# Sums of exponentials in the v products by constant columns beside v, and cluster masks of five score tiles on VectorE

## The chip, the cores and the metric

The kernel runs on one core of a Trainium2 chip. The metric is the device time of one execution in microseconds (us), the median of several runs. Traces come from one profiled execution. TensorE (PE) multiplies matrices, VectorE (DVE), ScalarE (ACT) and GpSimd (POOL) work on elements, SyncE (SP) and ScalarE issue DMAs.

## The reference

Attention restricted to clusters, and then a feed-forward layer. There are 4 batches, 8 heads, 768 positions, 64 values per head and 16 centroids per head.

```python
q_assign = argmax(q_n @ c_n)          # nearest of 16 centroids, per query
k_assign = argmax(k_n @ c_n)          # and per key
mask   = q_assign[..., :, None] == k_assign[..., None, :]
scores = where(mask, scale * (q @ k.T), -1e9)
attn   = exp(scores - max); attn = attn / (sum(attn) + 1e-9)
x      = (attn @ v) laid out as (3072 tokens, 512)
h = x @ w_in                          # 512 x 2048
out = (maximum(h, 0) ** 2) @ w_out    # 2048 x 512
```

## The kernel before

**Pairs of heads.** The attention part is a loop over `p`, 16 pairs of heads (4 batches x 4 pairs; `NG` is 16). The two heads of a pair are `e` = 0 and 1. Scores are kept transposed: keys on the 128 partitions, queries along the free axis. A pair has nine score tiles. Tiles 0 to 5 are the six blocks of 128 keys against the first 512 queries (`QA`), each for both heads, so 128x1024 numbers. Tiles 6 to 8 hold two key blocks each against the last 256 queries (`QB`). Score tiles stand in PSUM, in a pool `ps_sc` of three buffers that are reused in turn.

**A score tile.** `tile_of` takes a buffer (`begin`), issues the mask matmuls (`mask`, L450), which add nothing where the clusters of key and query agree and a huge negative number where they don't, adds the score matmuls on top (`score`, L441), and ScalarE takes the exponential into `ex` (`exponential`, L457). The operands of the mask matmuls are three bfloat16 rows per head (`rows_of`), made by VectorE in `number` from the logits to the centroids (`logits`, L329, and `turn_logits`, L340), sent to DRAM as `far` and read back (L377, L380).

**The v products.** `times_v` (L475) multiplies each block of keys' exponentials by v: the stationary operand is v of one head, 128 keys x 64, and the moving operand is `ex`, 128 keys x 512 or 256 queries. Head 0 writes to PSUM partitions 0 to 63 and head 1 to 64 to 127 of one bank, `V` for the first 512 queries and `M` for the last 256. ScalarE copies both into `xT` (`evict`, L484).

**The sums.** VectorE adds the nine tiles of exponentials into `total` (`add`, L460). TensorE multiplies `total` by a column of ones scaled by `UP` (`add_up`, L494), which sums over the keys. VectorE turns that and takes the reciprocal (`invert`, L503, L507), SP sends it to DRAM and reads it back broadcast over partitions (`far_r`, L509, and `rb`, L516), and VectorE multiplies `xT` by it in the next pair (`finish`, L539).

**What else runs in a pair.** q and k of later pairs are loaded, split into 16-bit words by ScalarE (`split_words`, L309), stored, and read back by a transposing DMA into `qkT` (`turn_words`, L321). One block of weights is loaded and rounded by ScalarE, VectorE and GpSimd (`round_1` to `round_3`).

**Order.** The order on every engine is written out by hand in the loop over `p` (`manual_schedule`): each engine executes what it is given in the order of the code. So an instruction that waits holds up all that stands behind it on its engine. SP's DMAs are such a queue too. Within a pair TensorE runs the nine score tiles, the products into `V`, those into `M`, the logits of a later pair, and the ones-matmuls.

**After the attention part.** The feed-forward layer follows, built from seven products in place of eight at up to two levels (L793, L883, L1003, L1111). It begins at 318.9 us of the trace. The last pair's sums are inverted and applied there, in `Rounding.behind`.

Of the kernel before, what the change touches and what calls it, by code (L numbers as in the profile page):

```python
# [25 lines left out]
def kernel(  # L26
# [40 lines left out]
    loads_v = att.enter_context(tc.tile_pool(name="loads_v", bufs=2))  # L67
    qktp = att.enter_context(tc.tile_pool(name="qktp", bufs=3))
    small = att.enter_context(tc.tile_pool(name="small", bufs=2))
    once = att.enter_context(tc.tile_pool(name="once", bufs=1))  # L70
    expp = att.enter_context(tc.tile_pool(name="expp", bufs=9))
    accp = att.enter_context(tc.tile_pool(name="accp", bufs=1))
# [6 lines left out]
    raw = {}  # L79
    raw_v = {}  # L80
# [13 lines left out]
    def load_v(pair):  # L94
        if pair >= NG:
            return
        b, hp = divmod(pair, HP)
        raw_v[pair] = loads_v.tile([P, 2, NCH, D], F32, name="v_raw")
        nc.sync.dma_start(
            raw_v[pair], v[b, 2 * hp : 2 * hp + 2].rearrange("h (p j) d -> p h j d", p=P)  # L100
        )
# [115 lines left out]

    seen = const.tile([P, NG * NBL], F32, name="seen")

    oh = accp.tile([P, NBL, 2, D], BF16, name="oh", tag="part")  # L220
# [120 lines left out]

    def number(pair):
        n = 2 * NBL
        mx = small.tile([P, n], F32, name="mx")
        best = once.tile([P, n, C], BF16, name="best")
        src = lt.pop(pair)

        def over_c(t):
            return t.unsqueeze(2).to_broadcast([P, n, C])

        nc.vector.reduce_max(out=mx, in_=src, axis=AX.X)
        nc.vector.tensor_tensor(out=best, in0=src, in1=over_c(mx), op=ALU.is_ge)
        nc.vector.tensor_tensor(
            out=best, in0=best, in1=order.unsqueeze(1).to_broadcast([P, n, C]), op=ALU.mult
        )
        nc.vector.reduce_max(out=mx, in_=best, axis=AX.X)
        if pair == 0:
            nc.vector.tensor_tensor(
                out=oh.rearrange("p b e c -> p (b e) c")[:, :, 0:C], in0=best, in1=over_c(mx),
                op=ALU.is_equal,  # L360
            )
            return
        squared = small.tile([P, n], F32, name="squared")
        nc.vector.tensor_tensor(out=squared, in0=mx, in1=mx, op=ALU.mult)
        for i, of in enumerate((squared, mx, squared)):
            nc.vector.tensor_scalar(
                out=marks[:, i, 0:n].rearrange("p (e b) -> p b e", e=2),
                in0=of.rearrange("p (b e) -> p b e", e=2), scalar1=factor[:, i : i + 1],
                scalar2=None if i == 1 else constant[:, i : i + 1], op0=ALU.mult,
                **({} if i == 1 else {"op1": ALU.add}),  # L370
            )
        turned = small.tile([P, 3, 32], BF16, name="marks_t")
        nc.vector.transpose(
            out=turned.rearrange("p f i -> p (f i)"), in_=marks.rearrange("p f i -> p (f i)")
        )
        far = dram.tile([3, 4, 32, 32], BF16, name="far")
        nc.sync.dma_start(far.rearrange("f g r i -> (g r) f i"), turned)  # L377
        rows = ohT[pair] = rows_of[pair % 2]
        for e in range(2):
            nc.sync.dma_start(  # L380
                rows[D * e : D * e + 3].rearrange("f w (g n) -> f (w g) n", g=2),
                far[:, :, NBL * e : NBL * (e + 1)].rearrange("f g b i -> f g (b i)"),
            )

# [35 lines left out]
    total = {}  # L420
    part = {}
# [14 lines left out]
    def score(pair, i, j, first):  # L436
        n = columns(i)
        c, cols = spots(i)[j]
        for e in range(2):
            rows = slice(D * e, D * (e + 1))  # L440
            nc.tensor.matmul(  # L441
                sc[i][:, e, cols], lhsT=qkT[pair][rows, NCH + c],
                rhs=qkT[pair][rows, n.start // P : n.stop // P], start=first, stop=not first,
            )
# [14 lines left out]
    def add(eng, out, a, b):  # L459
        eng.tensor_tensor(out=out, in0=a, in1=b, op=ALU.add)  # L460

# [9 lines left out]
    def times_v(pair, i, bank):  # L471
        n = columns(i)
        for c, cols in spots(i):
            for e in range(2):
                nc.tensor.matmul(  # L475
                    bank[D * e : D * (e + 1), 0 : n.stop - n.start], lhsT=raw_v[pair][:, e, c],
                    rhs=ex[i][:, e, cols], start=c == 0, stop=c == NCH - 1,
                )
        ex.pop(i)

    def evict(pair, i, bank):
        b, hp = divmod(pair, HP)
        n = columns(i)
        nc.scalar.copy(out=x_of(b)[:, hp, n], in_=bank[:, 0 : n.stop - n.start])  # L484

    spread_out = {}
    reciprocals = {}
    sums = {}

    def add_up(pair, bank):  # L490
        rows = P // 4
        for e in range(2):
            for g in range(2):
                nc.tensor.matmul(  # L494
                    bank[rows * (2 * e + g) : rows * (2 * e + g + 1), 0:TB], lhsT=ups[:, 0:rows],
                    rhs=total[pair][:, e, TB * g : TB * (g + 1)], start=True, stop=True,
                )
        total.pop(pair)
        sums[pair] = bank

    def invert(pair):
        turned = endp.tile([P, NBL, 32], F32, name="sums_t")
        nc.vector.transpose(  # L503
            out=turned.rearrange("p b i -> p (b i)"), in_=sums.pop(pair)[:, 0:TB]
        )
        r = seen[:, NBL * pair : NBL * (pair + 1)]
        nc.vector.reciprocal(out=r, in_=turned[:, :, 0])  # L507
        far = dram.tile([2, P // 2, NBL], F32, name="far_r")
        nc.sync.dma_start(far.rearrange("e i b -> (e i) b"), r)  # L509
        reciprocals[pair] = far  # L510

    def spread(pair):
        far = reciprocals.pop(pair)
        rb = endp.tile([P, 2, 32, NBL], F32, name="rb")
        for e in range(2):
            nc.sync.dma_start(  # L516
                rb[D * e : D * (e + 1)].rearrange("p g i b -> p (g i b)"),
                far[e].rearrange("i b -> (i b)").partition_broadcast(D),
            )
        spread_out[pair] = [rb[:, g] for g in range(2)]  # L520


    def spread_last(pair):
        far = reciprocals.pop(pair)
        spread_out[pair] = []
        for g in range(2):
            rb = outp.tile([P, DM], F32, name="rb_last", tag="osb")[:, 0:TB]
            for e in range(2):
                nc.sync.dma_start(
                    rb[D * e : D * (e + 1)],  # L530
                    far[e, 32 * g : 32 * (g + 1)].rearrange("i b -> (i b)").partition_broadcast(D),
                )
            spread_out[pair].append(rb.rearrange("p (i b) -> p i b", i=32))

    def finish(pair):
        b, hp = divmod(pair, HP)
        x = x_of(b)[:, hp].rearrange("p (g b i) -> p g b i", g=2, b=NBL)
        for g in range(2):
            nc.vector.scalar_tensor_tensor(  # L539
                out=x[:, g], in0=x[:, g], scalar=UP,  # L540
                in1=spread_out[pair][g].rearrange("p i b -> p b i"),
                op0=ALU.mult, op1=ALU.mult,
            )
        spread_out.pop(pair)
# [21 lines left out]
    def w_sums(i, odd=0):  # L566
# [8 lines left out]
        return a, s1, s2, s3, s4  # L575

# [36 lines left out]
    for p in range(NG):  # L613
# [3 lines left out]
        if p == HP + 1:  # L617
            nc.sync.dma_start(x_far[FEED[3]], xT.pop(FEED[3]))
        if p:
            invert(p - 1)  # L620
            if p == NG - 1:
                early_x_sums()
            turn_words(p + 2)
            spread(p - 1)
# [4 lines left out]
        if p:  # L629
            load_ahead(p - 1)  # L630

# [15 lines left out]
        else:  # L647
            for i in range(NB):
                tile_of(p, i)
        total[p] = endp.tile([P, 2, S], F32, name="total")  # L650
        first, last = total[p][:, :, 0:QA], total[p][:, :, QA:S]
        add(nc.vector, first, ex[0], ex[1])
# [6 lines left out]
        add(nc.vector, first, first, ex[2])  # L659
        for i in range(NB, NCH):  # L660
            if p != 1 or i > NB:
                tile_of(p, i)
            add(nc.vector, first, first, ex[i])
# [4 lines left out]
        else:  # L668
            split_words(p + 3, 0)
# [4 lines left out]
        part = accp.tile([P, 2, 512], F32, name="part")  # L674
        add(nc.vector, part, ex[NCH], ex[NCH + 1])
        add(nc.vector, part, part, ex[NCH + 2])
        add(nc.vector, last, part[:, :, 0:QB], part[:, :, QB : 2 * QB])
# [8 lines left out]
        round_1(p)  # L686


        for i in range(NCH):
            times_v(p, i, V)  # L690
        evict(p, 0, V)
        for i in range(NCH, NCH + NB):
            times_v(p, i, M)
        raw_v.pop(p)
        if p + 1 < NG:
            bank = begin("ls")
            if 2 < p + 2:
                if p + 2 < NG:
                    logits(p + 2, bank)
            add_up(p, bank[:, 1])  # L700
        evict(p, NCH, M)
# [630 lines left out]
    class Rounding:  # L1332
# [27 lines left out]
        def behind(self, i):  # L1360
            nonlocal wtp, spare_tile, four_r
            if i == 0:
                add_up(NG - 1, bank_tile(TB))
                invert(NG - 1)
                spread_last(NG - 1)
            if i == F2 - 2:
                finish(NG - 1)
                nc.sync.dma_start(x_far[FEED[2]], xT.pop(FEED[2]))
            if i == 5:
# [242 lines left out]
```

## Time and profile before

| | |
|---|---|
| median of 3 runs | 878.6 us (878.52 to 878.69) |
| profiled execution, its own time | 878.45 us |
| its span in the trace | 876.7 us |
| TensorE busy | 869.9 us, 99% |
| VectorE busy | 754.3 us, 86% |
| ScalarE busy | 385.8 us, 44% |
| GpSimd busy | 181.7 us, 21% |
| granted TensorE clock | 0.999 of full |
| from the first v product to the feed-forward part | 24.47 to 318.91 us |
| DMA engines busy in that stretch | 0.67 |

Busy times are sums over one execution. The span is what the trace covers; the execution's own time is 1.75 us longer. A row of the timeline gives a start, a duration, the engine, the line of the kernel, the operation, output and inputs by name with their sizes, and how many such instructions follow each other. A matmul's float32 product appears as two hardware passes, so that the trace shows twice as many as the program issues. Their durations overlap, so the rate is read from differences of starts. A row of a group gives busy time, mean duration in ns of one, and the idle time of the engine ahead of them with what ended it.

### The profile page before, as it was taken

Reading aid. Unit: us, or ns where it says so; the run is one execution under the profiler, and the core shown is the slowest. Engines: PE = TensorE matmul, PEld = TensorE weight load, DVE = VectorE, ACT = ScalarE, POOL = GpSimd, SP = SyncE. Lnnn points to the kernel's source line nnn. Section 1 sums busy time; section 2 is a strip of 40 time slices with the busy share of each in tenths; the row PEclk is TensorE's granted clock in tenths of the full one; section 3 lists DMA queues with packets and bytes.
Section 4 is the critical chain, followed back from the end, with each engine's and each line's share of the span. In section 5 each row is a group of like instructions: output and inputs, shape, how many; then the busy total and the mean of one; then the engine's idle time right before and its main releaser. Section 6 shows DMA issues by size and latency. Waiting matters only on the chain.

```text
span 876.7 us, 14996 instructions
## 1 busy us (share of the span) xinstructions
PE 869.9 (99%) x5487; PEld 597.4 (68%) x5487; DVE 754.3 (86%) x1359; ACT 385.8 (44%) x621; POOL 181.7 (21%) x240
## 2 busy tenths in 40 slices
PE   9999999999999999999999999999999999999997
PEld 5444444444444455568866689997767987779997
DVE  6799888888888999999858996797899898997786
ACT  5877667777765657750035430002453005440000
POOL 0000010000000246740056300005550064510000
PEclk9999999999999999999999999999999999999999
DMA  7777886767764235226701347681024740138663
GB/s 253 179 190 193 220 267 179 201 188 194 202 167 127 82 136 172 94 91 225 285 25 43 102 145 208 196 259 37 31 79 155 235 128 25 37 122 247 166 203 121
DMA packets 166402, 136.05 MB, mean 155 GB/s; under 512 B 58826, under 2 KB 140082, under 8 KB 166066
## 3 DMA queue, kind: packets, MB, share of 16 engines
q1 hardware_dynamic: 148018, 119.00, 46.1%
q10 hardware_dynamic: 18304, 16.03, 5.9%
q8 instruction: 45, 0.74, 0.3%
q14 instruction: 35, 0.29, 0.1%
HBM read 82.10 MB, written 41.89 MB: 141 GB/s over the span
## 4 chain that ended last, share of the span: by engine, by line
PE 99%; DMA 0%; ACT 0%; DVE 0%; issue 0%
PE bank L793 28%; PE bank L1111 25%; PE sc L441 14%; PE av_a L475 10%; PE bank L1003 6%; PE av_b L475 5%; PE sc L450 4%; PE bank L883 3%; PE sc L329 1%; PE more L883 1%; PE sc L494 1%; PE more L873 1%; DMA q_raw<-in_q_dram 0%; PE av_a L289 0%; ACT ex L457 0%; PE sc L274 0%
## 5 line engine op out<-in xcount | busy, mean ns | idle before, releaser
L457 ACT ACTIVATE ex<-sc 128x1024 f32<-128x1024 f32 x144 | 144.3, 1026 | 37.5 <-PE sc L441 31.6
L441 PE MATMUL sc<-qkT 64*128 64x512 f32 (+1 forms) x768 | 150.5, 484 | 0.0
L988 DVE TENSOR_TENSOR g<-bank,g 128x384 f32<-128x384 f32 (+3 forms) x205 | 102.3, 515 | 21.1 <-PE bank L793 12.8
L769 ACT ACTIVATE g<-g 128x384 f32<-128x384 f32 x122 | 62.9, 516 | 93.7 <-DVE g L988 73.5
L441 PEld LDWEIGHTS sc<-qkT 64*128 64x128 f32 x768 | 65.6, 188 | 42.1 <-issue 30.2
L793 PE MATMUL bank<-xT,w_s 128*128 128x384 f32 x256 | 93.1, 486 | 0.0
L793 PE MATMUL bank<-x_t,w_s 128*128 128x384 f32 x256 | 93.0, 486 | 0.0
L1267 ACT COPY spare<-bank 128x128 f32<-128x128 f32 x35 | 9.3, 264 | 187.7 <-PE bank L1111 163.8
L475 PE MATMUL av_a<-ex,v_raw 128*64 128x512 f32 x384 | 85.9, 596 | 0.0
L460 DVE TENSOR_TENSOR total<-total,ex 128x1024 f32<-128x1024 f32 x64 | 78.7, 1229 | 6.5
L161 POOL TENSOR_TENSOR w_in<-w_in,w_raw 128x512 int32<-128x512 int32 x16 | 21.4, 1337 | 293.9 <-DVE w_in L153 293.9
L571 POOL TENSOR_TENSOR w_s<-w_in 128x256 f32<-128x256 f32 x32 | 25.6, 800 | 247.4 <-PE bank L1111 146.4
L1111 PE MATMUL bank<-home,l 128*128 128x128 f32 x560 | 74.0, 275 | 0.0
L793 PEld LDWEIGHTS bank<-xT,w_s 128*128 128x128 f32 x256 | 48.6, 190 | 34.2 <-issue 0.5
L1111 PEld LDWEIGHTS bank<-home,l 128*128 128x128 f32 x560 | 68.2, 192 | 0.0
L793 PEld LDWEIGHTS bank<-x_t,w_s 128*128 128x128 f32 x256 | 48.1, 190 | 29.1
L793 PE MATMUL bank<-xT,w_in 128*128 128x384 f32 x184 | 67.1, 487 | 0.0
L770 ACT ACTIVATE g<-g 128x384 f32<-128x384 f32 x122 | 63.8, 523 | 3.9
L475 PEld LDWEIGHTS av_a<-ex,v_raw 128*64 128x64 f32 x384 | 26.2, 137 | 51.0 <-issue 49.3
L450 PE MATMUL sc<-rows 64*128 64x512 bf16 (+1 forms) x360 | 58.8, 323 | 0.0
L793 PEld LDWEIGHTS bank<-xT,w_in 128*128 128x128 f32 x184 | 34.4, 190 | 21.7 <-DVE g L551 0.6
L1111 PE MATMUL bank<-home,g 128*128 128x128 f32 x352 | 46.5, 275 | 0.0
(221 smaller groups left out, 1557.9 us busy)
## 6 DMA issues: line engine op xcount, KB each, us to landing
home<-w_far SPq DMA_DIRECT2D x92, 256.0 KB
words<-flat SPq DMA_DIRECT2D x26, 384.0 KB
w_raw<-in_moe_w_in_dram SPq DMA_DIRECT2D x16, 512.0 KB
w_raw<-in_moe_w_out_dram SPq DMA_DIRECT2D x16, 512.0 KB
w_far<-home SPq DMA_DIRECT2D x28, 256.0 KB
g<-g_far SPq DMA_DIRECT2D x28, 256.0 KB
v_raw<-in_v_dram SPq DMA_DIRECT2D x16, 384.0 KB
g_far<-third SPq DMA_DIRECT2D x24, 256.0 KB
```

What stands on the lines that cost most here:

```text
L441: nc.tensor.matmul(sc[i][:, e, cols], lhsT=qkT[pair][rows, NCH + c], rhs=qkT[pair][rows, n.start // P : n.stop // P], start=first, stop=no ...
L450: nc.tensor.matmul(sc[i][:, e, cols], lhsT=ohT[pair][rows, 1, c * P : (c + 1) * P], rhs=ohT[pair][rows, 0, columns(i)], start=first, stop= ...
L457: nc.scalar.activation(out=ex[i], in_=sc.pop(i), func=ACT.Exp, scale=SCALE)
L460: eng.tensor_tensor(out=out, in0=a, in1=b, op=ALU.add)
L475: nc.tensor.matmul(bank[D * e : D * (e + 1), 0 : n.stop - n.start], lhsT=raw_v[pair][:, e, c], rhs=ex[i][:, e, cols], start=c == 0, stop=c ...
L769: nc.scalar.activation(out=to, in_=to, func=ACT.Relu)
L770: nc.scalar.square(to, to)
L793: nc.tensor.matmul(bank, lhsT=operands[j][0][:, kk], rhs=operands[j][1][:, kk], start=(kk == 0), stop=(kk == H2 - 1),)
L883: nc.tensor.matmul(bank, lhsT=left, rhs=right, start=True, stop=True)
L988: nc.vector.tensor_tensor(out=out, in0=one, in1=two, op=ALU.add)
L1003: nc.tensor.matmul(bank, lhsT=left[j][:, f], rhs=right(j)[:, f], start=(f == 0), stop=(f == F2 - 1),)
L1111: nc.tensor.matmul(bank, lhsT=left[:, f], rhs=rhs[:, f], start=(f == 0), stop=(f == F4 - 1))
```

## The change

The v tiles of two alternate pairs become fixed buffers, `v_ups`. In them the 64 columns of v of each block of keys stand beside 64 columns that hold the constant `UP`, set once by GpSimd. A v product now takes 128 columns as its stationary operand: 64 rows of its output are the product, and the other 64 all hold the sum of the exponentials. Each head gets its own output. For the first 512 queries that is a buffer of `ps_sc`, with two heads side by side; for the last 256 it is `M`. `V` is used for the logits. The additions on VectorE, `total`, `part` and the ones-matmuls are gone.

`evict` copies both outputs to a tile `outputs` in SBUF. One row of sums per head goes to DRAM (`store_sums`), is read back as 128x12 (`load_sums`), inverted, stored, and broadcast as before. `finish` multiplies the product rows by it, per head, into `xT`.

From pair 2 on, tiles 0 to 4 get no mask matmuls. VectorE multiplies their exponentials by a comparison of the query's cluster (`of_queries`, the cluster numbers broadcast over the partitions) with the key's (`clusters`, one number per partition), one instruction per head and tile. SP loads both from `far` in the pair before (`load_clusters`), and ScalarE scales the keys' numbers (`scale_clusters`). Tiles 5 to 8, and all tiles of pairs 0 and 1, are masked by TensorE as before.

In the order: the word split of one operand moves behind the exponential of tile 6; the reciprocal moves behind `number` and the loads of v and weights; the last pair's `finish` comes one step earlier in the feed-forward part.

```diff
-    loads_v = att.enter_context(tc.tile_pool(name="loads_v", bufs=2))
+    v_ups = [once.tile([P, 2 * NCH * P + P], F32, name=f"v_ups_{i}") for i in range(2)]
...
-        nc.sync.dma_start(
-            raw_v[pair], v[b, 2 * hp : 2 * hp + 2].rearrange("h (p j) d -> p h j d", p=P)
-        )
+        raw_v[pair] = v_ups[pair % 2]
+        for e in range(2):
+            at = e * (NCH * P + D)
+            halves = raw_v[pair][:, at : at + NCH * P].rearrange("p (c d) -> p c d", d=P)
+            nc.sync.dma_start(
+                halves[:, :, 0:D], v[b, 2 * hp + e].rearrange("(p j) d -> p j d", p=P)
+            )
...
+    for t in v_ups:
+        for at in (D, NCH * P):
+            in_front = t[:, at : at + NCH * P].rearrange("p (c d) -> p c d", d=P)
+            nc.gpsimd.memset(in_front[:, :, 0:D], UP)
...
+    def load_clusters(pair):
+        far = far_marks.pop(pair)
+        for e in range(2):
+            for g in range(2):
+                n = min(TB, QA - TB * g)
+                nc.sync.dma_start(
+                    of_queries[:, e, TB * g : TB * g + n],
+                    far[1, g, NBL * e : NBL * e + n // 32].rearrange("b i -> (b i)")
+                    .partition_broadcast(P),
+                )
+        of_keys[pair] = small.tile([P, 2 * HANDS], BF16, name="of_keys")
+        for e in range(2):
+            for g in range(2):
+                c = slice(NB * g, min(NB * (g + 1), HANDS))
+                nc.sync.dma_start(
+                    of_keys[pair][:, HANDS * e + c.start : HANDS * e + c.stop],
+                    far[1, 2 + g, NBL * e : NBL * e + P // 32 * (c.stop - c.start)]
+                    .rearrange("(c b) i -> (b i) c", b=P // 32),
+                )
+
+    def scale_clusters(pair):
+        clusters[pair] = small.tile([P, 2, HANDS], F32, name="clusters")
+        nc.scalar.activation(
+            out=clusters[pair].rearrange("p e c -> p (e c)"), in_=of_keys.pop(pair),
+            func=ACT.Copy, scale=0.5 / BIG,
+        )
...
-    def times_v(pair, i, bank):
-        n = columns(i)
+    def times_v(pair, i, e, bank):
         for c, cols in spots(i):
-            for e in range(2):
-                nc.tensor.matmul(
-                    bank[D * e : D * (e + 1), 0 : n.stop - n.start], lhsT=raw_v[pair][:, e, c],
-                    rhs=ex[i][:, e, cols], start=c == 0, stop=c == NCH - 1,
-                )
+            at = (e * NCH + c) * P
+            nc.tensor.matmul(
+                bank, lhsT=raw_v[pair][:, at : at + P], rhs=ex[i][:, e, cols],
+                start=c == 0, stop=c == NCH - 1,
+            )
...
-    def add_up(pair, bank):
...
+    def store_sums(pair):
+        sums[pair] = dram.tile([2, S], F32, name="sums")
         for e in range(2):
+            row = D * (1 - e)
+            nc.sync.dma_start(sums[pair][e : e + 1], outputs[pair][row : row + 1, e])
+
+    def load_sums(pair):
+        compact[pair] = small_c.tile([P, NBL], F32, name="compact")
+        nc.sync.dma_start(
+            compact[pair], sums.pop(pair).rearrange("e (i b) -> (e i) b", b=NBL)
+        )
...
+    def tile_by_hand(pair, i):
+        begin(i)
+        score(pair, i, 0, True, True)
+        exponential(i)
+        for e in range(2):
+            nc.vector.scalar_tensor_tensor(
+                out=ex[i][:, e], in0=of_queries[:, e], scalar=clusters[pair][:, e, i : i + 1],
+                in1=ex[i][:, e], op0=ALU.is_equal, op1=ALU.mult,
+            )
...
         if p:
-            invert(p - 1)
-            if p == NG - 1:
-                early_x_sums()
+            load_sums(p - 1)
             turn_words(p + 2)
-            spread(p - 1)
         if 2 < p + 1 < NG:
             turn_logits(p + 1)
             number(p + 1)
         load_v(p + 1)
         if p:
             load_ahead(p - 1)
+
+        if p:
+            invert(p - 1)
+            spread(p - 1)
...
+        if BY_HAND <= p + 1 < NG:
+            load_clusters(p + 1)
+
+        bank = begin("av")
+        for i in range(NCH):
+            for e in range(2):
+                times_v(p, i, e, bank[:, e])
         round_1(p)
...
+        evict(p, slice(0, QA), sc.pop("av"))
+        both = M.rearrange("p (e n) -> p e n", e=2)
+        for e in range(2):
+            for i in range(NCH, NCH + NB):
+                times_v(p, i, e, both[:, e])
+        ex.clear()
         raw_v.pop(p)
-        if p + 1 < NG:
-            bank = begin("ls")
-            if 2 < p + 2:
-                if p + 2 < NG:
-                    logits(p + 2, bank)
-            add_up(p, bank[:, 1])
-        evict(p, NCH, M)
+        if 2 < p + 2 < NG:
+            sc["ls"] = V.rearrange("p (a n) -> p a n", a=1)
+            logits(p + 2, sc["ls"])
+        evict(p, slice(QA, S), both)
+        store_sums(p)
```

## The prediction

> **What bounds the kernel now.** I read the page first: the busy row and the chain that ended last.
>
> ```profile
> PE 869.9 (99%) x5487; PEld 597.4 (68%) x5487; DVE 754.3 (86%) x1359; ACT 385.8 (44%) x621; POOL 181.7 (21%) x240
> PEclk9999999999999999999999999999999999999999
> PE 99%; DMA 0%; ACT 0%; DVE 0%; issue 0%
> ```
>
> TensorE is busy for 99% of the span, its granted clock is full in every slice, and the chain is TensorE from end to end. Every us put on TensorE is a us of the span, and work taken from VectorE alone is worth nothing. Next I read TensorE's timeline over one steady pair of heads (the pair that starts after the logits at 166.51):
>
> ```profile
> 157.55 0.60 PE L441 MATMUL sc<-qkT 64*128 64x256 f32 x4
> 163.82 2.76 PE L475 MATMUL av_b<-ex,v_raw 128*64 128x256 f32 x24
> 166.51 0.85 PE L329 MATMUL sc<-qkT,cnT 128*32 128x384 f32 x8
> 167.18 0.83 PE L494 MATMUL sc<-total,ups 128*32 128x384 f32 x8
> 167.94 0.39 PE L450 MATMUL sc<-rows 64*128 64x512 bf16 x2
> 168.17 1.02 PE L441 MATMUL sc<-qkT 64*128 64x512 f32 x4
> 169.03 0.38 PE L450 MATMUL sc<-rows 64*128 64x512 bf16 x2
> 177.75 5.37 PE L475 MATMUL av_a<-ex,v_raw 128*64 128x512 f32 x24
> 182.95 2.76 PE L475 MATMUL av_b<-ex,v_raw 128*64 128x256 f32 x24
> 185.64 0.85 PE L329 MATMUL sc<-qkT,cnT 128*32 128x384 f32 x8
> ```
>
> Durations overlap at their ends, so I take differences of starts. The period is 185.64-166.51 = 19.13 us: logits 0.67, sums (L494) 0.76, nine score tiles with masks 167.94 to 177.75 = 9.81, v products 5.20 + 2.69 = 7.89. Without gaps.
>
> **The v products, +121 us.** The program issues as many v matmuls after as before (twelve of 512 and twelve of 256 columns a pair, each shown as two passes, so 24 and 24). What changes is the stationary operand, 128x64 before and 128x128 after. Before, 24 passes of 512 columns take 5.20 us, 0.217 each, and 24 of 256 take 2.69, 0.112 each. The same trace has float32 passes with a 128x128 stationary operand in the feed-forward part:
>
> ```profile
> 385.98 1.45 PE L793 MATMUL bank<-xT,w_in 128*128 128x384 f32 x4
> 387.27 1.45 PE L793 MATMUL bank<-xT,w_s 128*128 128x384 f32 x4
> 392.43 7.07 PE L1003 MATMUL bank<-w_out,g 128*128 128x256 f32 x32
> 399.33 2.97 PE L1003 MATMUL bank<-w_t,g_s 128*128 128x256 f32 x13
> ```
>
> (399.33-392.43)/32 = 0.2156 us for 256 columns and (387.27-385.98)/4 = 0.3225 for 384: 0.107 for 128 more, so 0.429 for 512 (estimate by that line). A full-width pass costs nearly twice what a half-width one does. So the two heads' products, which go to PSUM partitions 0-63 and 64-127, share the array in time today; with 128 columns each they can't. After: 24 x 0.429 + 24 x 0.2156 = 10.31 + 5.17 = 15.48 us, +7.59 a pair, x 16 = +121.4.
>
> Here a rule has to be weighed. The Trainium skill, "TensorE: Matmul & The Clock Gate", section "Step-by-step: what each phase is for", says that columns of the moving operand enter one per cycle and "this is why throughput is purely `N cycles`". Taken alone, the constant columns ride free: this term is 0 and the edit a gain of 27 us (below). The rows above decide against it for this case. The rule that fits them, and speaks against the change, is in "TensorEngine Tiling (Array Packing)", section "When to Use Tiling": a stationary operand of at most 64 columns allows 2x column tiling. The change gives that factor up.
>
> **What TensorE saves, -27 us.** The mask matmuls of tiles 0 to 4 go for pairs 2 to 15: a 512-column pair of them spaces L450 to L441 by 168.17-167.94 = 0.23 at the first and 0.21 at the next tiles; I take 0.215 x 5 x 14 = 15.05. The ones-matmuls of L494 go in all 16 pairs (the last one's stood in the feed-forward part, 328.13 to 328.92): 0.76 x 15 + 0.79 = 12.2. Sum for TensorE: 121.4 - 15.05 - 12.2 = +94.2. The steady pair becomes 19.13 + 7.59 - 1.08 - 0.76 = 24.9 us.
>
> **VectorE and ScalarE.** These are the rows:
>
> ```profile
> L460 DVE TENSOR_TENSOR total<-total,ex 128x1024 f32<-128x1024 f32 x64 | 78.7, 1229 | 6.5
> L145 DVE SCALAR_TENSOR_TENSOR w_raw<-w_raw 128x512 uint32<-128x512 uint32 x16 | 11.0, 689 | 0.0
> L457 ACT ACTIVATE ex<-sc 128x1024 f32<-128x1024 f32 x144 | 144.3, 1026 | 37.5 <-PE sc L441 31.6 <-DVE mx L351 0.9 <-ACT flat L309 0.5
> ```
>
> VectorE loses seven additions of about 1.22 and one of 0.69 a pair (9.3 us) and the transpose of the sums (0.58). It gains ten scalar_tensor_tensor of 128x512, nearest row L145 at 0.69, so 6.9. The mix with a bfloat16 operand isn't in the trace: 0.55 (the 128x384 compare) to 1.2 bounds it, 0.69 taken. finish() becomes two of 64x768, about 1.0 each against 0.84. VectorE ends with some 16 of 24.9 us: its relief is worth nothing, as it wasn't the bound. ScalarE: nine exponentials 9.2, words 3.2, rounding 1.4, evictions 1.03 + 0.59 (both heads' full width), one small scaling (0.2): 15.6 of 24.9. In the five unmasked tiles TensorE needs only 0.86 a tile and ScalarE 1.03, with three score buffers. From the pair's start: exponential 0 begins at 1.5, exponential 6, whose buffer the first v products now need, ends near 8.9; TensorE has its last score at 0.67 + 8.73 = 9.4. Hidden, with 0.5 us in hand. The move of the first word split behind exponential 6 is after that point. The four memsets of the constants on GpSimd (2 to 5 us by its rows of 0.5 to 1.3 each) run before the first v product at 24.5.
>
> **Queues and new waits.** The sums now go ScalarE eviction, DRAM (2 stores), compact (1 load), reciprocal, DRAM, broadcast; the clusters go through 4 broadcasts and 4 loads of single 2-byte values; v is loaded by 2 DMAs in 256-byte pieces. All are on SP, whose issue times the timeline shows:
>
> ```profile
> 168.95 0.34 SPq L509 DMA_DIRECT2D far_r<-seen  x1
> 170.11 3.48 SPq L321 DMA_TRANSPOSE qkT<-words  x1
> 173.70 1.16 SPq L516 DMA_DIRECT2D rb<-far_r  x2
> 177.99 1.53 SPq L380 DMA_DIRECT2D rows<-far  x2
> SPq L380 <- DMA far<-marks_t: 39.8, 15, 3.6
> ```
>
> A pair's issues on SP add up to 9.0 us now. New ones: sums and compact 3 x 0.34, broadcasts 4 x 0.58, keys 4 x 0.4 to 0.8 (0.55 taken), v 0.38: 5.9, so 14.9. SP also stops for three round trips through DRAM where it stopped for one (rb's was hidden under the transpose): 3 x 2.65 (39.8/15). That is 22.9 us, begun 0.8 after the pair's start, and the last keys land 2.65 later, at 26.3; scale_clusters of the next pair stands on ScalarE ahead of its exponential 0, due at 24.9 + 1.5 = 26.4. No margin. A second loop is as tight: rb lands, finish() reads `outputs` (one buffer), then ScalarE may evict the next products. The Trainium skill, "DMA: Bandwidth & Descriptors", section "Anatomy of one DMA — SWDGE (gpsimd) path", gives a fixed cost of about 2.0 us per DMA: by it SP is through 2 us earlier and nothing shows. The trace's 2.65 on this queue (up to 3.6) is what I use; at 3.6 each the pair grows by about 2.5 to 3 us. I take 0.5 us for 13 pairs, 6.5; bounds 0 and 39 (below 0 there is nothing, as TensorE's own sum stays).
>
> Sum: 94.2 + 6.5 = +100.7. The profiled execution's own time is 878.45 us (span 876.7 and 1.75 around it), 0.15 below the median of 878.6. 878.6 + 100.7 = 979.3, given as 979.
>
> **The rivals.**
> - SP's chain through DRAM becomes the bound: 1 to 3 us more in 13 pairs, +13 to +39 over 94.2: 986 to 1012, middle 998. For it: the sums above have no margin, and the DMA engines are about 0.7 busy in this part while the change adds some 3,000 small packets a pair. Against: a DMA stall of one pair may be taken up by the next, and the last pairs have no words to turn.
> - The hand masks come late: the reciprocal stands ahead of them on VectorE and waits for compact. At 2.65 a trip compact lands near 7.2, the first mask is done near 8.8, needed at 9.4; at 3.6 a trip it is 1.3 us late, x 14 = 18: 991.
> - Faster: the array runs a 128-column float32 pass in the time of a 64-column one. Then -27.2, 851. It decides from an extra below 1.7 us a pair (27.2/16). Against it are the L1003 and L793 rows; only another cause of their slowness would save it.
> - The change doesn't do what it says: the instruction order shows full-width products, no L494, and ten VectorE masks a pair, so I give this nothing.
>
> **How the numbers follow.** As forecast (969 to 986) 0.62; SP chain 0.22; late masks 0.13; faster 0.02; no change 0.01. The range 969 to 1004 begins a little under TensorE's sum without a stall (878.6 + 94.2 = 972.8) and takes in all but the worst of the SP case. Faster by over 0.2%, about what a measurement here can tell, 0.02; within 0.2% 0.01; slower 0.97.
>
> **What would show it.** Right: v products at 0.43 and 0.215 us a pass, 15.5 us a pair, steady pair near 25 us, TensorE still nearly full. If passes are at 0.22 and 0.11 the main step is wrong. ScalarE waiting for of_keys, or TensorE idle ahead of the first v product for VectorE's masks, are the two stall cases, seen in the waits.

## The result, and the profile after

The changed kernel takes 990.0 us (median of 4 runs, 988.63 to 991.65) against 878.64: the ratio is 1.127, 95% interval 1.1245 to 1.1287. The forecast was 979, range 969 to 1004. The span of the profiled execution, the fastest of the four, grew from 876.7 to 986.8 us. The page of the changed kernel, the same rows as in the prediction:

```profile
PE 972.6 (99%) x5219; PEld 680.4 (69%) x5219; DVE 701.1 (71%) x1355; ACT 390.5 (40%) x635; POOL 180.5 (18%) x244
PEclk9999999999999999999999999999999999999999
PE 85%; DMA 5%; DVE 4%; SPq 2%; issue 2%; ACT 1%; ACTq 0%; DVEq 0%
```

TensorE still fills 99% of the span at full clock, with 268 fewer recorded instructions but 103 us more of work. VectorE went from 86% to 71%: relief on an engine that wasn't the bound. New is that DMA, SP and VectorE have a share in the chain of waits: in places TensorE now waits for something.

TensorE's timeline of one pair of the changed kernel, the one with the longest stall (start, duration, instruction; a bracket gives idle time ahead):

```profile
157.05 10.57 PE L513 MATMUL sc<-ex,v_ups 128*128 128x512 f32 x24
167.46 5.34 PE L513 MATMUL av_b<-ex,v_ups 128*128 128x256 f32 x24
172.73 0.85 PE L338 MATMUL av_a<-qkT,cnT 128*32 128x384 f32 x8
173.51 2.85 PE L482 MATMUL sc<-qkT 64*128 64x512 f32 x12
179.04 2.04 PE L482 MATMUL sc<-qkT 64*128 64x512 f32 x8 [2.68 <-ACT ex L499]
180.92 0.38 PE L492 MATMUL sc<-rows 64*128 64x512 bf16 x2
185.35 10.57 PE L513 MATMUL sc<-ex,v_ups 128*128 128x512 f32 x24
```

Differences of starts: 24 passes of 512 columns take 167.46-157.05 = 10.41 us, 0.434 each on average; 24 of 256 take 5.27, 0.220 each. Together they are 15.68 us, where the kernel before had 7.89. The next pair's fourth score tile waits 2.68 us for an exponential. Pairs without such a wait take 25.29 us from one first v product to the next; this one takes 28.30.

Who is late is seen on ScalarE and SP in the same stretch (two views of the changed kernel):

```profile
172.95 1.01 ACT L527 COPY outputs<-sc 128x1024 f32<-128x1024 f32 x1 [9.54 <-PE av_b L513]
173.86 0.59 ACT L527 COPY outputs<-av_b 128x512 f32<-128x512 f32 x1
177.87 0.21 ACT L423 ACTIVATE clusters<-of_keys 128x10 f32<-128x10 bf16 x1 [3.42 <-DMA of_keys<-far]
177.98 6.49 ACT L499 ACTIVATE ex<-sc 128x1024 f32<-128x1024 f32 x7
```

```profile
167.56 1.45 SPq L553 DMA_DIRECT2D rb<-far_r  x2
169.11 1.12 SPq L319 DMA_DIRECT2D words<-flat  x2
170.32 3.15 SPq L406 DMA_DIRECT2D of_queries<-far  x4
173.52 2.00 SPq L415 DMA_DIRECT2D of_keys<-far  x4
175.61 0.56 SPq L534 DMA_DIRECT2D sums<-outputs  x2
```

ScalarE waits 3.42 us for the keys' clusters, and the seven exponentials stand behind that wait. SP issues those loads last in its round, at 173.52, when TensorE is already at the next pair's scores; and the sums' stores come behind them at 175.61 although the sums were there at 174.5. SP's round up to these stores began with those of the pair before, at 148.16, and took 27.45 us, longer than TensorE's own 25.29; the next one takes 26.27. What stretched this round most is one transposing load (the second row is the next pair's):

```profile
150.17 5.56 SPq L330 DMA_TRANSPOSE qkT<-words  x1
178.01 3.33 SPq L330 DMA_TRANSPOSE qkT<-words  x1
```

From pair 2 to pair 13 the issue of that load takes 2.70 to 3.96 us in all pairs but this one. Why it took 5.56 here was not looked into.

TensorE's waits over the whole of the changed kernel (us in all, number of waits, the longest):

```profile
PE sc L482 <- ACT ex L499: 4.1, 4, 2.7
PE sc L513 <- issue: 2.9, 1, 2.9
```

The second is pair 0's first v product, at 28.52 in place of 24.47.

### The profile page after: what moved, and what is told of

It is laid out like the page before. It is cut to its first block, busy times and chain, and to the rows that moved or that the text cites. A ratio compares the mean times of both kernels' runs of the same rounds, so it can differ in the third digit from the quotient of the medians.

```text
span 986.8 us, 14642 instructions
## 1 busy us (share of the span) xinstructions
PE 972.6 (99%) x5219; PEld 680.4 (69%) x5219; DVE 701.1 (71%) x1355; ACT 390.5 (40%) x635; POOL 180.5 (18%) x244
## 4 chain that ended last, share of the span: by engine, by line
PE 85%; DMA 5%; DVE 4%; SPq 2%; issue 2%; ACT 1%; ACTq 0%; DVEq 0%
PE bank L1147 22%; PE bank L829 19%; PE sc L513 14%; PE sc L482 11%; PE av_b L513 7%; PE bank L1039 5%; PE bank L919 2%; DMA far_r<-seen 2%; PE sc L492 1%; PE more L919 1%; DVE g L786 1%; DVE w_raw L154 1%; DVE w_raw L150 1%; DMA of_keys<-far 1%; PE av_a L338 1%
## 5 line engine op out<-in xcount | busy, mean ns | idle before, releaser
L513 PE MATMUL sc<-ex,v_ups 128*128 128x512 f32 x384 | 169.0, 597 | 2.9 <-issue 2.9
L482 PE MATMUL sc<-qkT 64*128 64x512 f32 (+1 forms) x768 | 144.8, 490 | 4.1 <-ACT ex L499 4.1
L499 ACT ACTIVATE ex<-sc 128x1024 f32<-128x1024 f32 x144 | 137.3, 1038 | 7.0 <-PE sc L482 5.8
L513 PEld LDWEIGHTS sc<-ex,v_ups 128*128 128x128 f32 x384 | 71.7, 190 | 92.4 <-issue 87.9
L560 DVE SCALAR_TENSOR_TENSOR xT<-outputs,rb 64x768 f32<-64x768 f32 x32 | 31.1, 970 | 123.4 <-DMA rb<-far_r 123.0
L602 DVE SCALAR_TENSOR_TENSOR ex<-of_queries,clusters,ex 128x512 f32<-128x512 bf16 x140 | 93.1, 740 | 0.3 <-issue 0.3
L513 PE MATMUL av_b<-ex,v_ups 128*128 128x256 f32 x384 | 85.5, 379 | 0.0
L513 PEld LDWEIGHTS av_b<-ex,v_ups 128*128 128x128 f32 x384 | 73.0, 190 | 16.7 <-issue 7.7
```

Source lines behind the costliest of these rows:

```text
L482: nc.tensor.matmul(sc[i][:, e, cols], lhsT=qkT[pair][rows, NCH + c], rhs=qkT[pair][rows, n.start // P : n.stop // P], start=first, stop=no ...
L499: nc.scalar.activation(out=ex[i], in_=sc.pop(i), func=ACT.Exp, scale=SCALE)
L513: nc.tensor.matmul(bank, lhsT=raw_v[pair][:, at : at + P], rhs=ex[i][:, e, cols], start=c == 0, stop=c == NCH - 1,)
L560: nc.vector.scalar_tensor_tensor(out=x_of(b)[rows, hp], in0=o[rows, e], scalar=UP, in1=rb[rows], op0=ALU.mult, op1=ALU.mult,)
L602: nc.vector.scalar_tensor_tensor(out=ex[i][:, e], in0=of_queries[:, e], scalar=clusters[pair][:, e, i : i + 1], in1=ex[i][:, e], op0=ALU.i ...
```

## The experiments

The theory: the 128-column stationary operand costs nearly all of it, and two small stalls come on top (clusters late through SP; pair 0's word splits). The rivals: the new chains and queues make the time, not the width; or the masks do.

**The width alone, on the kernel before.**

```diff
-                    bank[D * e : D * (e + 1), 0 : n.stop - n.start], lhsT=raw_v[pair][:, e, c],
...
+            at = (e * NCH + c) * D - D * e
+            nc.tensor.matmul(
+                bank, lhsT=raw_v[pair].rearrange("p h c d -> p (h c d)")[:, at : at + P],
...
+        for e in range(2):
+            rows = slice(D * e, D * (e + 1))
+            nc.scalar.copy(out=x_of(b)[rows, hp, cols], in_=bank[rows, e])
```

> The kernel before with only the v products widened: each takes 128 columns as its stationary operand (v of the block and 64 columns that stand beside it in the same tile), each head writes all 128 partitions of its own output, and ScalarE copies only the 64 rows that are wanted. The additions, the ones-matmuls and the mask matmuls stay, and the first word split stands behind the exponential of tile 6, as in the changed kernel. If the width of the stationary operand is what costs, the passes take 0.434 and 0.220 us as in the changed kernel, 15.68 us a pair for 7.89: 16 x 7.79 = +125, and some 4 us at pair 0, where the products wait for the exponential of tile 6 behind the word splits: 1004 to 1012. If the width is free and the changed kernel's time comes from its longer chains and queues, this one stays within a few us of 879.

Measured: 1007.17 us, ratio 1.145 (1.143 to 1.147). The v products and TensorE's waits:

```profile
108.89 10.57 PE L474 MATMUL sc<-ex,v_raw 128*128 128x512 f32 x24
119.30 5.34 PE L474 MATMUL av_b<-ex,v_raw 128*128 128x256 f32 x24
124.57 0.85 PE L329 MATMUL sc<-qkT,cnT 128*32 128x384 f32 x8
PE sc L474 <- ACT ex L457: 2.9, 1, 2.9
```

Again 10.41 and 5.27 us, and no wait in any pair but the first. This kernel has none of the change's sums and masks. It does have what goes with the wide products: a score buffer as their output, the head-by-head order for the last 256 queries, and the moved word split. It costs more than the whole change, 128 us against 111, each over the kernel before as timed in its own session, so the rest of the change gives some 16 us back. The wait at pair 0 is named here: the exponential whose buffer the products take.

**The width undone, on the changed kernel.**

```diff
-                bank, lhsT=raw_v[pair][:, at : at + P], rhs=ex[i][:, e, cols],
+                bank[D * e : D * (e + 1)], lhsT=raw_v[pair][:, at + D * e : at + D * (e + 1)],
+                rhs=ex[i][:, e, cols],
```

> The changed kernel with 64-column v products again, head 0 to partitions 0 to 63 and head 1 to 64 to 127. The sums are therefore missing; product rows go through the same stores and loads in their place and a constant is used as reciprocal, by an operation of the same size. ScalarE evicts the two heads by two copies of 64 partitions each in place of one. If the width is what costs, passes return to 0.217 and 0.112 us and TensorE's work falls by 7.8 us a pair to 17.5. Then either nothing else bounds, and the time is 990 - 125 = 865; or SP's chain (stores, loads and three trips through DRAM a pair, 23 to 25 us by the forecast's sum) takes over, pairs stay at 23 to 26 us with TensorE idle for 6 us and more of each, and the time is 950 to 990. I expect the second. If the width isn't the cause the passes stay near 0.43.

Measured: 961.3 us, ratio 1.093 (1.091 to 1.095). TensorE's timeline, its waits, ScalarE's wait, and three stretches of time. A row of a stretch gives its length, the busy time and number of instructions of TensorE, its weight loads, VectorE, ScalarE and GpSimd, then the granted clock (1.00, 0.57, 1.00) and the DMA engines' share and GB/s:

```profile
179.36 5.37 PE L513 MATMUL sc<-ex,v_ups 128*64 128x512 f32 x24
184.56 4.54 PE L513 MATMUL av_b<-ex,v_ups 128*64 128x256 f32 x24
189.03 0.85 PE L338 MATMUL av_a<-qkT,cnT 128*32 128x384 f32 x8
196.17 3.65 PE L482 MATMUL sc<-qkT 64*128 64x512 f32 x8 [3.51 <-ACT ex L499]
199.65 0.38 PE L492 MATMUL sc<-rows 64*128 64x512 bf16 x2
PE sc L482 <- ACT ex L499: 40.2, 14, 4.2
ACT clusters L423 <- DMA of_keys<-far: 35.4, 14, 5.6
189.10:196.00 6.90, 3.56 (x20) 1.07 (x20) 6.53 (x15) 3.01 (x6) 1.28 (x1) 1.00 0.48 76
196.00:200.00 4.00, 3.83 (x12) 1.66 (x14) 3.87 (x8) 3.04 (x5) 0.00 (x0) 0.57 0.99 203
200.00:204.00 4.00, 4.00 (x42) 2.45 (x38) 2.98 (x5) 3.89 (x5) 0.00 (x0) 1.00 0.14 33
```

Three readings. The 512-column passes are back at 5.20/24 = 0.217 us: it is the width. The 256-column passes are at 4.47/24 = 0.186, not the 0.112 I expected: the change runs all of head 0 and then all of head 1 there, so that most neighbours write to the same half of PSUM's partitions, and those don't share the array (rows below). And the time falls by 29 us only, as SP's round now sets the pair (from pair 2 to 12 mostly 23.8 to 27.8 us between first v products, with one of 21.5; about 21 after that). TensorE waits 40 us in 14 waits for exponentials. These stand behind the cluster loads, for which ScalarE waits 35.4 us, and behind evictions that themselves come late (7.7 us more of TensorE's waits). After 3.5 us of idling the granted clock was 0.57, and eight score passes took 3.48 us against 1.88 at full clock.

Two neighbouring passes of 256 columns show the sharing itself: in the kernel before, in the changed kernel, and with the width undone. A row gives the start of the first and the time until the end of the second; one pass alone lasts 0.38 us in all three.

```profile
182.95 0.39 PE L475 MATMUL av_b<-ex,v_raw 128*64 128x256 f32 x2
167.89 0.60 PE L513 MATMUL av_b<-ex,v_ups 128*128 128x256 f32 x2
184.78 0.59 PE L513 MATMUL av_b<-ex,v_ups 128*64 128x256 f32 x2
```

Before, the passes of the two heads start 0.01 us apart and run side by side, and the next two start 0.21 us later. With 128 columns a pass starts 0.22 us after the other. With 64 columns head by head it is 0.21 too; only in the middle of the 24, where head 1 follows head 0, some passes overlap, which gives the 0.186. So a wide pass takes no longer than a narrow one that runs alone. What the change gives up is two at a time. Narrow products in turns were not tried on the changed kernel. The rival of longer weight loads falls with this: they take 0.137 us for 64 columns and 0.190 for 128, and passes of the last two rows follow each other equally fast.

**The masks alone, on the kernel before**, with the functions of the change for tiles 0 to 4 and nothing else.

```diff
+                        scale_clusters(p)
+                    tile_by_hand(p, i)
...
+            load_clusters(p + 1)
```

> The kernel before with only the masks of tiles 0 to 4 moved to VectorE for pairs 2 to 15, and the loads of the clusters; additions, ones-matmuls and narrow v products stay. TensorE's pair falls from 19.13 to 18.05 us. VectorE has 17.5 us of work a pair in the kernel before and gets 6.7 more (ten instructions as measured in the changed kernel): 24.2, so VectorE becomes the bound and 14 pairs take about 5 us more each: 945 to 960. The rival, that the masks lie beside TensorE's work and only the saved matmuls count, gives 864.

Measured: 951.56 us, ratio 1.083 (1.081 to 1.084). TensorE's waits, and busy times in one pair (VectorE's is the third):

```profile
PE sc L478 <- DVE lt L340: 18.6, 13, 1.6
PE av_a L513 <- DVE ex L620: 18.1, 23, 1.6
PE sc L478 <- ACT ex L495: 6.1, 3, 3.6
151.51:175.40 23.89, 20.85 (x126) 9.87 (x126) 23.20 (x37) 13.57 (x18) 1.28 (x1) 1.00 0.67 167
```

VectorE is the bound: its transposes of the sums start at 151.51, 175.40 and 199.28, 23.9 us apart, it is busy for 23.2 us of that, and TensorE waits for its masks and transposes. ScalarE waits for the keys here too (50.8 us in all), but VectorE has no idle time from that. In the kernel before, VectorE has no room for five masks. So the two halves of the change belong together (the constant columns free VectorE, the masks use it), but together they buy about 1 us of TensorE's masks and 0.76 of its ones-matmuls in each pair of heads for 7.8 us of its products.

**All masks on TensorE, on the changed kernel** (`BY_HAND = NG`).

> The changed kernel with all masks on TensorE again: no cluster loads (8 DMAs a pair fewer on SP), no scaling on ScalarE, no masks on VectorE. TensorE gets 15 us more. If the stalls of pairs 3 to 14 (6 us) come from the cluster loads at the end of SP's queue, they go: 990 + 15 - 6 = 999, and TensorE waits only at pair 0. If they come from the chain of the sums (broadcast of the reciprocals, one outputs buffer), they stay: 1005.

Measured: 998.02 us, ratio 1.135 (1.133 to 1.137). TensorE waits 2.9 us at pair 0 and in no later pair, although the broadcast reciprocals come late:

```profile
DVE xT L560 <- DMA rb<-far_r: 208.0, 15, 16.9
```

VectorE waits 208 us for them and TensorE for none of it. So with the cluster loads gone the sums' own loop, which the forecast had called as tight as the clusters', costs TensorE nothing. With them SP has less time for it, and it does cost something ("Both mends"). A pair takes 26.27 us here and 25.29 in the changed kernel, so TensorE's masks of five tiles are 0.98 us.

**The cluster loads on ScalarE's queue.** `load_clusters` issues on `nc.scalar` in place of `nc.sync`, behind `round_1`.

> The changed kernel with the eight cluster loads of a pair issued by ScalarE behind its rounding and ahead of its eviction of the first products, in place of SP. ScalarE has about 15.6 us of work in a pair of 25.3, and the issues take some 5. If the 6 us that TensorE loses in pairs 3 to 14 come from SP being late with the clusters, most of it goes: 984 to 986. The rival, that the transfers themselves are late (DMA engines too busy with small packets), leaves the stalls: 990. If ScalarE can't take 5 us more, its evictions come late and it is over 990.

Measured: 1002.89 us, ratio 1.142 (1.140 to 1.144): worse. ScalarE's timeline:

```profile
224.40 6.24 ACTq L406 DMA_DIRECT2D of_queries<-far  x4
230.68 2.05 ACTq L415 DMA_DIRECT2D of_keys<-far  x4
232.85 1.01 ACT L527 COPY outputs<-sc 128x1024 f32<-128x1024 f32 x1 [9.98 <-DMA of_queries<-far]
```

The issues hold ScalarE for 8 us, and the eviction of the products stands behind them. This trial moved the hold-up and says nothing on why the loads are late.

**The scaling on VectorE.** The loads stay; only the instruction that waits for them moves.

```diff
-        nc.scalar.activation(
-            out=clusters[pair].rearrange("p e c -> p (e c)"), in_=of_keys.pop(pair),
-            func=ACT.Copy, scale=0.5 / BIG,
+        nc.vector.tensor_scalar(
+            out=clusters[pair].rearrange("p e c -> p (e c)"), in0=of_keys.pop(pair),
+            scalar1=0.5 / BIG, scalar2=None, op0=ALU.mult,
```

> The changed kernel with the clusters scaled by VectorE ahead of its first mask, in place of ScalarE ahead of its first exponential. The loads stay where they were and land as late as before. If TensorE's 6 us in pairs 3 to 14 come from the exponentials that stand behind the scaling on ScalarE, they go, as VectorE's first mask is needed only some 8 us later: 984. If the clusters come so late that the masks are late too, or the sums' loop limits, less or nothing is gained: 988 to 990.

Measured: 986.08 us (985.09 to 987.69), ratio 1.122 (1.120 to 1.124). TensorE's waits for exponentials fall from 4.1 to 0.3 us, so it is mostly the place of the waiting instruction that turned late loads into a stall. The gain is 4 us, two less than I expected, at a scatter of the runs of 2.6.

**Pair 0's word splits behind the exponential of tile 6.**

> The changed kernel with pair 0's word splits moved behind the exponential of tile 6, as the change does for the other pairs. If TensorE's 2.9 us ahead of the first v product are the wait for that exponential (its score buffer is the one that the products take), they go: 987. If they are a wait for v or the constants, nothing changes: 990.

Measured: 987.53 us (985.69 to 989.93), ratio 1.1235 (1.122 to 1.125). By the times alone that is not apart from the changed kernel; by the profile, TensorE's 2.9 us at the first v product are gone.

**Both mends.**

> Both mends of the changed kernel: scaling on VectorE, and pair 0's word splits behind the exponential of tile 6. If the two stalls are all that TensorE loses beside its own longer work, 990 - 6 - 2.9 = 981, TensorE idle for about as long as in the kernel before (7 us of the span), and what is left, some +102, is the width of the v products less the matmuls saved. If time is hidden elsewhere, it stays at 984 or more.

Measured: 981.94 us (981.41 to 982.15), ratio 1.117 (1.115 to 1.118). TensorE's longest waits, and the one place where it still loses most:

```profile
PE sc L184 <- DVE zeros L181: 1.1, 1, 1.1
PE bank L1147 <- DVE g L570: 0.7, 1, 0.7
PE sc L482 <- ACT ex L499: 0.5, 2, 0.3
193.72 0.95 DVE L560 SCALAR_TENSOR_TENSOR xT<-outputs,rb 64x768 f32<-64x768 f32 x1 [0.97 <-DMA rb<-far_r]
194.83 1.02 ACT L527 COPY outputs<-sc 128x1024 f32<-128x1024 f32 x1 [8.64 <-DMA words<-flat]
```

Little is left in TensorE's waits, and the scatter fell from 3.0 to 0.7 us. Three periods still exceed 25.29 us, by 1.8 in all. The last two rows show why. `finish` waits for the broadcast reciprocals and ends at 194.67, and the eviction into the one buffer that `finish` reads starts at 194.83. The row names another releaser, but in the changed kernel and in this one the eviction starts 0.15 to 0.16 us after `finish` ends in every pair from 2 to 14. This is the sums' loop: by these times it is the next to bind once the clusters no longer do; no run took it away. 103 us of slowdown remain; TensorE's busy time is 101.3 us above the kernel before's (971.2 against 869.9).

**One tile masked on VectorE, on the kernel before**: was there anything to gain on the good side? First with the scaling on ScalarE, then on VectorE.

> The kernel before with the mask of tile 0 alone on VectorE, pairs 2 to 15. TensorE saves 14 x 0.215 = 3.0 us: 876, if VectorE has room. VectorE's pair grows from 17.5 to 18.9 us, TensorE's falls from 19.13 to 18.92. The rival is that VectorE, now as long as TensorE, makes TensorE wait where it reads a score buffer late (as five masks do, 18.6 us of waits for the transpose of the logits): 880 to 886.

> The kernel before with the mask of tile 0 alone on VectorE, now with the cluster numbers scaled by VectorE too. If its 24 us over the kernel before came from ScalarE waiting for the cluster loads ahead of the exponentials, it falls to 876 to 880, perhaps 3 us under the kernel before (14 x 0.215 us of TensorE saved). If VectorE, with 19.0 us in a pair of 18.9, is the bound, or if the loads hold up SP's other work, it stays above: 882 to 900.

Measured: 902.6 us, ratio 1.027 (1.024 to 1.030), and 892.06 us, ratio 1.0145 (1.012 to 1.017). Neither rival of the first was right: it was not VectorE that held TensorE up but again ScalarE's scaling (52.9 us of waits for the keys), and moving it gives back 10 us. In the second, SP's `of_queries` issues take 4.8 to 5.1 us a pair, and VectorE runs nearly without a gap (from 100 to 290 us it waits 5.8 us for the keys and hardly for anything else), with TensorE waiting for it:

```profile
PE sc L488 <- DVE lt L340: 4.9, 6, 1.3
PE sc L532 <- DVE total L498: 0.8, 2, 0.5
```

I found no version that beats the kernel before. How much of the 13 us left is VectorE and how much SP was not separated.

## Why the prediction was right, point by point

- **What bounds**: right. TensorE stayed at 99% and decided.
- **Where 990 lies**: inside the range, but by its number alone in the 986 to 1012 given to SP's chain, beside the 991 of late masks, and not in the 969 to 986 of the forecast's own course. The profile shows that neither rival came true: stalls of 6.0 us and not 13 to 39, and masks in time. The span grew by 110.1 us and not by 100.7, by the terms below: 3.2 more for the products, about 3 for logits and scores, 4.05 up to the first product, and 0.5 less for stalls.
- **v products**: forecast 0.429 and 0.216 us a pass and +7.59 a pair; measured 0.434 and 0.220 on average and +7.79, so +124.6 in place of +121.4. Within a group the passes do start 0.43 and 0.216 us apart, as forecast from the 384- and 256-column rows of the feed-forward part; what was left out is about 0.1 us where each group begins. The width was shown twice, by adding it (1007) and by undoing it (512-column passes at 0.217).
- **The rule weighed**: by the Trainium skill's "purely `N cycles`" ("TensorE: Matmul & The Clock Gate", section "Step-by-step: what each phase is for") alone the term would have been 0, as the number of passes stays the same. For a single pass the traces don't contradict it: 256 columns take 0.21 to 0.22 us with a narrow and with a wide stationary operand. What it leaves out is that two narrow passes ran in that time. The prediction inferred this from rates, and the starts of the passes show it.
- **Saved matmuls**: the steady pair without a wait is 25.29 us, forecast 24.9. Of the 0.4, 0.2 is the v products, 0.1 the logits (0.78 for 0.67) and 0.1 the score tiles (8.83 for 8.73, as five tiles of masks are worth 0.98 us and not 1.08).
- **Stalls of the clusters**: forecast 0.5 us a pair, 6.5 in all, by SP's round ending just at ScalarE's due time. The periods of the v products exceed 25.29 by 6.0 us in sum from pair 3 on (3.0 in one, 0.1 to 0.9 in six, none in the rest). That 6.0 meets 6.5 is in part luck. Half of it fell on one pair, behind one long transposing load. Moving the scaling took away 4.2 to 4.4 of it, and the rest came back as the sums' loop. The terms, too, were less good than their sum: SP's wait for `far_r` was 4.1 us on average (65.1/16), for `far` 2.1 and for the sums 1.0, where each was put at 2.65; the v loads took 0.65 an issue and not 0.38, the query broadcasts 0.79 and not 0.58. The fixed 2.0 us weighed in the prediction stands for DMAs issued by GpSimd; these three waits of SP lie on both sides of it.
- **Late masks**: no, but not by much. Ten masks took 6.7 us (forecast 6.9), and even in the pair with the longest stall they ran 179.59 to 186.30 against the first product at 185.35. The closest is the pair whose first product starts at 157.05: the two masks of tile 0 ended at 156.69.
- **What failed** is "Hidden, with 0.5 us in hand" for exponential 6, with the word splits after it. That holds from pair 1 on. In pair 0 they stand ahead of it (two copies of each operand, 3.1 us of ScalarE), and the first products now take the buffer that this exponential frees: 2.9 us of wait. The first v product comes 4.05 us later in all. The other 1.1 us are lost before pair 0's scores, whose masks begin at 16.34 and not at 15.29; in the traces of other variants with the same code up to there they begin between 15.47 and 16.19, so this part varies from trace to trace and is not shown to be the change's. The step was worked out for the steady pair and not for the first.

Sum: 124.6 for the products, -27.3 for the saved matmuls as forecast, 6.0 for the stalls, 4.05 up to the first product, about 3 for the slower logits and scores: 110.4, against 110.1 in the span.

## What to carry to other kernels

A constant column beside an operand is free only while it doesn't change how the array is shared: look for rows of both widths in the trace, and for passes that start together, before counting the extra columns at nothing. Work taken from an engine that isn't the bound pays for nothing; price the trade in the bound engine's us. And where a load may be late, put the instruction that waits for it on the engine whose next work is due latest, and check a moved step at the first turn of the loop as well as in the steady one.

## What the runs showed of the hardware beyond that

- Half-width float32 passes of 256 columns took 0.112 us on average in turns of two heads (PSUM partitions 0-63 and 64-127, starting 0.01 us apart), 0.186 head by head, and full-width ones 0.220.
- With the width undone, TensorE's granted clock was 0.57 in the 4 us that followed 3.5 us of idling, and 1.00 again after that; in the changed kernel, which keeps TensorE busy, it was 1.00 over the span.
- Four query-cluster issues hold an issuing engine for 3.15 us on SP in the changed kernel and up to 6.24 on ScalarE, in part perhaps by waits inside. Such issues have to be counted as work of that engine.
